# A dilated three-tap convolution with a gated activation: other operands for the warm-up products, and work pulled ahead of four places where TensorE waits

## The chip, the cores and the metric

The kernel runs on one core of a Trainium2 chip. The metric is the time of one execution on the device in microseconds (us), as the median of three runs. A core has TensorE (PE, the matrix products), VectorE (DVE), ScalarE (ACT), GpSimd (POOL), SyncE (SP, which issues most of the DMAs) and 16 DMA engines. Each engine works through its own list of instructions in order and waits on semaphores for the others.

## The reference

```python
def reference(x, w, w_o):          # x (2, 16000, 256), w (3, 256, 512), w_o (256, 256), all bf16
    dil = 2
    pad = (K - 1) * dil
    xp = jnp.pad(x, ((0, 0), (pad, 0), (0, 0)))
    h = jnp.einsum('btc,cd->btd', xp[:, pad:pad + T, :], w[0])
    for i in range(1, K):
        off = pad - i * dil
        h = h + jnp.einsum('btc,cd->btd', xp[:, off:off + T, :], w[i])
    f, g = h[..., :D], h[..., D:]
    z = jnp.tanh(f) * jax.nn.sigmoid(g)
    return z @ w_o
```

Every output row is made of three products of rows of `x` that lie two apart with a 256 x 512 weight, a tanh of one half times a sigmoid of the other, and one more product with a 256 x 256 weight.

## The kernel before

The time axis is cut into groups of rows. Most groups are wide: 256 columns of 8 rows each, read transposed by a DMA into a tile `xq`. A group is worked off in four blocks of 128 output channels, in the order 0, 2, 1, 3, so that a tanh block and its sigmoid block follow each other. The main loop goes over the blocks by number `k`; it starts at `k = ND = 4`, since blocks 0 to 3 belong to a first small group that is computed directly. There is also a small group `extra` (tiles `xte`, `e_ps`), whose four blocks are strewn into the loop at `k` = 4 to 7 by `extra_block`, and a small group `end` (`f_ps`).

The wide blocks save products. VectorE (and GpSimd for a part) first forms sums and differences of the input columns (`q`, `qp`, `qm`, `qd`), and each block then needs seven pairs of 512-column products. A block's PSUM tile `y` has two banks, and its steps follow each other across engines:

- `first` (weights `wmh`, two products, one for each half `ct` of the input channels) and ScalarE's copy `st` of the sum (`keep_first`),
- `second` (weights `wph`) and ScalarE's copy `sv` (`keep_second`), from which GpSimd makes `other`,
- `third` (weights `wm`), after which VectorE splits the bank into the second one (`split_bank`, L286),
- `late(B, 0)` in the next turn (weights `wt`, `wu`), which needs the split; then VectorE's `rest` (L290, `sv<-sv,y`), which needs these products,
- `late(B, 1)` (weights `wd2`, `wd0`, operand `qd`), which adds to the banks that `rest` has read and so needs `rest`,
- the activations on ScalarE, the gate (tanh times sigmoid, L339) on VectorE, and in a later turn the output products `out_mm` (L364), ScalarE's copy out of PSUM (L401) and the store.

`y` tiles come from a pool of three, the tiles `o_ps`, `e_ps` and `f_ps` from a pool of two. The order on each engine is the order of the calls in the loop; nothing is rescheduled. VectorE's steps other than `split_bank` and `rest` come from three tables by `k`: `small` and `big`, run early in a turn, and `mid`, which holds one step alone, `wide_m(G, 1)` of the second wide group at `k = 7`, which forms the second half of `qm` for the block that comes next.

At the start TensorE has no data yet. It runs products on a tile `warm` that VectorE sets to zero, L140, until the first 512 rows of `x` have come. These are transposed on TensorE (`turn`, L183) and copied to SBUF; from then on real products run (`direct`, L310), and VectorE forms the weight sums and the first `q`, `qp` and `qm`.

At the end of the list there are no blocks left to fill the waits: `late(V, 0)` of the last block, the projections that are left over (`project`, `left`), `late(V, 1)`, and the last group's projections, whose stores are issued one after the other by SP and ScalarE.

Of the kernel before, what the change touches and what calls it, by code (L numbers as in the profile page):

```python
# [13 lines left out]
def kernel(  # L14
# [23 lines left out]
    nc = tc.nc  # L38
    bf16 = mybir.dt.bfloat16
# [3 lines left out]
    P = 128  # L43
# [6 lines left out]
    BANK = 512  # L50
    O_ORDER = (0, 2, 1, 3)
    TAPS = (2, 0, 1)
# [4 lines left out]
    for b in range(B):  # L57
        t, stop = (4 * 2 * P if b == 0 else 0), (T - 4 * RE if b == B - 1 else T)
        while t < stop:
            n = min(need, (stop - t) // 8)  # L60
# [14 lines left out]
    consts = ctx.enter_context(tc.tile_pool(name="consts", bufs=1))  # L75
# [22 lines left out]

    def load_plain(G):
        b, r0, R = G["b"], G["r0"], G["R"]  # L100
# [22 lines left out]
            G["cols"].append((col + RH, slice(row, row + rows)))  # L123
            col, row = col + RH + rows, row + rows

    warm = consts.tile([P, BANK], bf16)
    nc.vector.memset(warm[:], 0.0)
    w_taps = [consts.tile([P, CT, D2], bf16, name=f"w{k}_sb") for k in range(K)]
    wo_sb = consts.tile([P, NT, D], bf16)
    xn = osb_pool.tile([P, 4, D], bf16, name="osb")  # L130
# [3 lines left out]
        nc.scalar.dma_start(out=w_taps[k][:], in_=w_in[k])  # L134
    nc.scalar.preload_act_table(ACT.Sigmoid)
    nc.sync.dma_start(out=w_taps[TAPS[1]][:], in_=w_in[TAPS[1]])
    for n in range(14):
        if n < 6 and n % 2 == 0:
            wps = new_y()
        nc.tensor.matmul(  # L140
            wps[:, 1, (n % 2) * 256:(n % 2 + 1) * 256], lhsT=warm[:, :P], rhs=warm[:, :256],
            start=n % 2 == 0 and n < 6, stop=True, skip_group_check=True,
        )
# [107 lines left out]
    def first(B, ct):  # L251
        if ct == 0:
            B.y = new_y()
        nc.tensor.matmul(  # L254
            B.y[:, 0, :], lhsT=W["wmh"][:, ct, B.osl], rhs=B.G["qp"][:, :, ct, :],
            start=ct == 0, stop=ct == CT - 1, skip_group_check=True,
        )
# [4 lines left out]
    def third(B):  # L262
        mm(B, W["wm"], B.G["qm"][:, 1], 0)

    def late(B, n):
        G = B.G
        if n == 0:
            mm(B, W["wt"], G["q"][:, 1, 0], 0)
            mm(B, W["wu"], G["q"][:, 1, 1], 1)
        else:  # L270
            mm(B, W["wd2"], G["qd"][:, 0], 0)
            mm(B, W["wd0"], G["qd"][:, 1], 1)
# [12 lines left out]
    def split_bank(B):  # L285
        nc.vector.scalar_tensor_tensor(  # L286
            out=B.y[:, 1, :], in0=B.st[:], scalar=-0.5, in1=B.y[:, 0, :], op0=ALU.mult, op1=ALU.add)
# [67 lines left out]
            return G["z"][:, dt, WIDE_PLACE[jp], lo:lo + P]  # L355
        return G["z"][:, dt, 2 * jp + q, rb0:rb0 + P]

    def out_mm(G, rb0, jp, o_ps=None):
        if o_ps is None:
            o_ps = ps_o.tile([P, 2, D], f32, name="o_ps", tag="o_ps")  # L360
        G["o", rb0, jp] = o_ps
        for q in range(2):
            for dt in range(NT):
                nc.tensor.matmul(  # L364
                    o_ps[q] if isinstance(o_ps, list) else o_ps[:, q, :], lhsT=z_columns(G, rb0, jp, q, dt), rhs=wo_sb[:, dt, :],
                    start=(dt == 0), stop=(dt == NT - 1),
                )

    def store(G, rb0, js, osb, queue=None):

        queue = queue or nc.sync
        if not G["wide"]:
            t0 = 4 * G["r0"] + 4 * rb0
            queue.dma_start(out=out[G["b"], t0:t0 + 4 * P, :].rearrange("(p j) d -> p j d", j=4)[:, js, :], in_=osb[:])
            return
        row = 0
        for b, t0, rows in G["parts"]:
            lo, hi = max(rb0, row), min(rb0 + P, row + rows)
            if lo < hi:
                t = t0 + 8 * (lo - row)  # L380
                queue.dma_start(
                    out=out[b, t:t + 8 * (hi - lo), :].rearrange("(p j) d -> p j d", j=8)[:, js, :],
                    in_=osb[lo - rb0:hi - rb0],
                )
            row += rows

    def out_evict(G, rb0, jp, on_dve):
        o_ps = G["o", rb0, jp]
        copy = nc.vector.tensor_copy if on_dve else nc.scalar.copy
        if jp is None:  # L390
            te = 4 * G["r0"]
            osb = consts.tile([P, 2, D], bf16, name="osb_end")
            copy(out=osb[:], in_=o_ps)
            rows = out[G["b"], te:te + 4 * RE, :].rearrange("(r q h) d -> h r q d", q=2, h=2)
            for h in range(2):
                nc.sync.dma_start(out=rows[h], in_=osb[h * RE:(h + 1) * RE])
            return
        h = jp % 2
        if h == 0:
            G["osb"] = osb_pool.tile([P, 4, D], bf16, name="osb")  # L400
        copy(out=G["osb"][:, 2 * h:2 * h + 2, :], in_=o_ps)  # L401
        if h == 1:
            store(G, rb0, slice(2 * jp - 2, 2 * jp + 2), G["osb"])


    blocks = [Block(G, oi) for G in groups for oi in range(4)]
    extras = [Block(extra, oi) for oi in range(4)]
    ends = [Block(end, oi) for oi in range(4)]
    ND = 4
# [47 lines left out]
    last = wide_m(G0, 1)  # L457

    def extra_block(i, taps):
        E = extras[i]  # L460
        if TAPS[0] in taps:
            E.y = ps_o.tile([P, BANK], f32, name="e_ps", tag="o_ps")
        direct(E, taps, E.y[:])
        if TAPS[-1] in taps:
            activate(E, E.y[:])
# [17 lines left out]
    ready, todo, made = [], [], []  # L483
    small, big, mid = {}, {}, {}

    def do(steps, k):
        ins = None
        for step in steps.pop(k, []):
            ins = step() or ins
        return ins  # L490
# [32 lines left out]
    def project(n):  # L523
        for piece in todo[:n]:
            out_mm(*piece)
            made.append(piece)
        del todo[:n]

    for k in range(ND, NB):
        B, V = blocks[k], (blocks[k - 1] if k > ND else None)  # L530

        E = {
            ND: [(0, TAPS[2:]), (1, TAPS[:1])], ND + 1: [(1, TAPS[2:])], ND + 2: [(2, TAPS)],
            ND + 3: [(3, TAPS)],
        }.get(k, [])
        early_second = k == ND + 1
        if early_second:
            second(B)
            keep_second(B)
            extra_block(1, TAPS[1:2])  # L540
        if V:
            late(V, 0)
        if k >= ND + 2:
            Y = blocks[k - 2]
            activate(Y, "y")
            note_gates(Y, k)
        last = do(small, k) or last

        if k == ND + 6:
            todo.append(ready.pop())  # L550
        big_late = k == ND + 1

        def big_and_quarter(last):
            last = do(big, k) or last
            if B.oi == 0 and k > ND:
                quarter(B.G, 3, last)
            elif B.oi and not big_late and B.G["n"] + 1 < len(wides):
                for i in range(0 if k == ND + 2 else B.oi - 1, B.oi):
                    quarter(wides[B.G["n"] + 1], i, last)
            return last  # L560

        if not big_late:
            last = big_and_quarter(last)
        if not early_second:
            second(B)
            keep_second(B)
        if k == ND:
            for i in range(2, ND):
                activate(blocks[i], bank(blocks[i], i))
        other(B, last)  # L570
        if V:
            rest(V)
        last = do(mid, k) or last
        for e in E:
            extra_block(*e)
        if k in (ND + 4, ND + 5):
            plain_ends(*((ACT.Sigmoid, 1) if k == ND + 5 else (ACT.Tanh, 0)))

        project(0 if k < ND + 3 else 1 if k < ND + 6 else 2)
        evict()  # L580
        N = blocks[k + 1] if ND < k < NB - 1 else None

        split_first = k >= ND + 2
        if N:
            first(N, 0)
            if not split_first:
                first(N, 1)
        third(B)
        split_bank(B)
        if k == ND + 3:  # L590
            last = gates_of(extra, slice(0, 2))
        if big_late:
            last = big_and_quarter(last)
        if V:
            activate(V, "sv")
        if N:
            if split_first:
                first(N, 1)
            keep_first(N)
        if V:  # L600
            late(V, 1)
        todo += ready
        ready.clear()
        if B.oi == 0:
            if loaded_wide < len(wides):
                load_wide(loaded_wide)
                loaded_wide += 1
            if k == ND:
                load_end()
# [2 lines left out]

    Y, V = blocks[NB - 2:]
    G = V.G
    late(V, 0)
    activate(Y, "y")
    big.pop(NB)
# [5 lines left out]
    gate_phases(0, slice(0, 2), nc.gpsimd)  # L623
    rest(V)
    gate_phases(0, slice(2, 4))
    project(2)
    evict()


# [5 lines left out]
    left = [todo[i:i + 2] for i in range(0, len(todo), 2)]  # L635
# [17 lines left out]

    activate(V, "sv")
    two_pieces(left[0], "y")
    out_evict(*left[0][0], True)
    late(V, 1)
    gate_phases(1, slice(2, 4))
    activate(V, "y")
    out_evict(*left[0][1], True)  # L660
    two_pieces(left[1], "o")
    last_mm(0, (1, 2), "y")
    gate_phases(1, slice(0, 2))
    out_evict(*left[1][0], False)
    out_evict(*left[1][1], False)
    last_mm(P, (1, 2), "y")
    last_evict(0, (1, 2), (nc.sync, nc.sync))
    last_mm(0, (0, 3), "o")
# [35 lines left out]
```

## Time and profile before

| | |
|---|---|
| median of three runs | 263.51 us (263.49 to 263.56) |
| the profiled execution | 263.43 us, of which the span from the first to the last instruction 261.6 us |
| PE busy | 256.0 us, 98% of the span |
| ACT busy | 245.9 us, 94% |
| DVE busy | 226.7 us, 87% |
| POOL busy | 112.8 us, 43% |
| chain of work that ended last | PE 93%, DVE 3% |

The median is 0.08 us above the profiled execution, and 1.8 us of that execution lie outside the span. A product's recorded time runs from its start to its end and overlaps that of the next one, so a busy share of 98% does not say how dense the products are. The gaps between the starts do.

### The profile page before, as it was taken

How to read it: one execution, taken by the hardware profiler on the slowest of the kernel's cores; microseconds unless marked ns; L12 is line 12 of the kernel's file. 1: busy time of each engine (PE TensorE's matmuls, PEld its weight loads, DVE VectorE, ACT ScalarE, POOL GpSimd, SP SyncE). 2: the span in 40 equal slices, each digit the busy share in tenths (PEclk: the TensorE clock that was granted, in tenths of full speed). 3: DMA queues.
4: the chain of work that ended last, by engine and by line, in shares of the span. 5: the costliest groups of instructions: out<-in, count | busy, mean ns of one | idle time of the engine just before them, and what ended most of it. 6: DMA issues, size and time to landing. Idle time of an engine off the chain costs nothing.

```text
span 261.6 us, 4231 instructions
## 1 busy us (share of the span) xinstructions
PE 256.0 (98%) x1464; PEld 144.2 (55%) x1464; DVE 226.7 (87%) x264; ACT 245.9 (94%) x378; POOL 112.8 (43%) x129
## 2 busy tenths in 40 slices
PE   8999999999999999999999999999999999999993
PEld 6644555555555555555555555555555555555562
DVE  2989969989889989999988988988988988986673
ACT  4668789999999999999999999999999999999993
POOL 1033434454453454355455355355345345444240
PEclk9999999999999999999999999999999999999998
DMA  7979073292834719256392934729274491221226
GB/s 209 201 177 192 0 180 94 83 209 83 175 119 123 209 52 212 111 117 174 96 175 105 199 120 103 203 79 215 81 169 124 101 231 43 80 83 40 82 80 241
DMA packets 79109, 35.10 MB, mean 134 GB/s; under 512 B 69232, under 2 KB 71536, under 8 KB 79088
## 3 DMA queue, kind: packets, MB, share of 16 engines
q1 hardware_dynamic: 77984, 33.92, 52.8%
q10 hardware_dynamic: 1104, 0.92, 1.1%
q8 instruction: 11, 0.18, 0.3%
q14 instruction: 10, 0.08, 0.1%
HBM read 1.18 MB, written 16.38 MB: 67 GB/s over the span
## 4 chain that ended last, share of the span: by engine, by line
PE 93%; DVE 3%; issue 1%; DMA 1%; ACT 0%; DVEq 0%; ACTq 0%
PE y L246 58%; PE o_ps L364 19%; PE y L254 9%; PE y L310 2%; PE y L140 1%; PE e_ps L310 1%; PE f_ps L310 1%; DVE sv L290 1%; DVE y L286 1%; DMA out_dram<-osb 1%; DVE qm L222 1%; PE wt_ps L171 0%; ACT osb L401 0%; PE y L364 0%; DVE osb L648 0%
## 5 line engine op out<-in xcount | busy, mean ns | idle before, releaser
L283 POOL TENSOR_TENSOR sv<-sv,st 128x512 f32<-128x512 f32 x60 | 76.4, 1274 | 23.9 <-ACT sv L280 22.2
L231 POOL TENSOR_TENSOR qd<-xq 128x256 bf16<-128x256 bf16 (+2 forms) x60 | 34.9, 585 | 114.2 <-DVE zw L339 55.4
L290 DVE TENSOR_TENSOR sv<-sv,y 128x1024 f32<-128x1024 f32 x60 | 72.7, 1212 | 3.8 <-PE y L246 3.7
L246 PE MATMUL y<-qd,wd_sb 128*128 128x512 bf16 x240 | 61.6, 379 | 0.1
L401 ACT CAST osb<-o_ps 128x512 bf16<-128x512 f32 x114 | 61.1, 591 | 0.2 <-PE o_ps L364 0.2
L286 DVE SCALAR_TENSOR_TENSOR y<-st,y 128x512 f32<-128x512 f32 x60 | 41.8, 696 | 21.9 <-PE y L246 19.6
L364 PE MATMUL o_ps<-wo_sb,zw 128*128 128x256 bf16 x450 | 58.4, 273 | 0.0
L364 PEld LDWEIGHTS <-zw 128*128 128x128 bf16 x480 | 47.0, 98 | 17.1
L254 PE MATMUL y<-qp,wmh_sb 128*128 128x512 bf16 x120 | 44.8, 379 | 0.0
L246 PEld LDWEIGHTS <-wd_sb 128*128 128x128 bf16 x240 | 23.5, 98 | 28.5 <-issue 0.6
L280 ACT ACTIVATE sv<-y 128x512 f32<-128x512 f32 x60 | 35.9, 598 | 1.4 <-PE y L246 1.1
L213 DVE TENSOR_TENSOR q<-xq 128x2048 bf16<-128x2048 bf16 (+2 forms) x32 | 36.8, 1155 | 0.0
L276 ACT ACTIVATE st<-y 128x512 f32<-128x512 f32 x60 | 36.3, 607 | 0.2 <-PE y L254 0.2
L246 PE MATMUL y<-q,wt_sb 128*128 128x512 bf16 x120 | 35.7, 379 | 0.2 <-DVE y L286 0.2
L246 PE MATMUL y<-qm,wph_sb 128*128 128x512 bf16 x120 | 35.7, 379 | 0.0
L246 PE MATMUL y<-qm,wm_sb 128*128 128x512 bf16 x120 | 35.7, 379 | 0.0
L246 PE MATMUL y<-q,wu_sb 128*128 128x512 bf16 x120 | 35.7, 379 | 0.0
L339 DVE TENSOR_TENSOR zw<-thw,sgw 128x2048 bf16<-128x2048 bf16 x28 | 34.1, 1217 | 0.0
L332 ACT ACTIVATE thw<-sv 128x1024 bf16<-128x1024 f32 x30 | 32.4, 1078 | 0.4 <-DVE sv L290 0.4
L332 ACT ACTIVATE sgw<-sv 128x1024 bf16<-128x1024 f32 x30 | 32.4, 1078 | 0.0
L334 ACT ACTIVATE sgw<-y 128x1024 bf16<-128x1024 f32 x30 | 31.3, 1043 | 0.1
L334 ACT ACTIVATE thw<-y 128x1024 bf16<-128x1024 f32 x30 | 31.3, 1044 | 0.0
(68 smaller groups left out, 178.8 us busy)
## 6 DMA issues: line engine op xcount, KB each, us to landing
out_dram<-osb SPq DMA_DIRECT2D x56, 256.0 KB, 2.1
out_dram<-osb SPq DMA_DIRECT2D x6, 128.0 KB, 2.2
w_sb<-in_w_dram ACTq DMA_DIRECT2D x2, 256.0 KB, 4.4
out_dram<-osb SPq DMA_DIRECT2D x2, 160.0 KB, 2.0
osb<-in_x_dram SPq DMA_DIRECT2D x1, 256.0 KB, 3.2
w_sb<-in_w_dram SPq DMA_DIRECT2D x1, 256.0 KB, 4.3
xq<-in_x_dram SPq DMA_TRANSPOSE x16, 7.2
out_dram<-osb ACTq DMA_DIRECT2D x2, 128.0 KB, 2.2
```

The source lines that it names most:

```text
L213: ins = nc.vector.tensor_tensor(out=sums(G, "q")[:, h, :, :, :, sl].rearrange("p h q ct r -> p h (q ct) r"), in0=s, in1=a, op=ALU.subtract ...
L246: nc.tensor.matmul(B.y[:, bank, :], lhsT=wmat[:, ct, B.osl], rhs=mv[:, :, ct, :], start=False, stop=ct == CT - 1, skip_group_check=True,)
L254: nc.tensor.matmul(B.y[:, 0, :], lhsT=W["wmh"][:, ct, B.osl], rhs=B.G["qp"][:, :, ct, :], start=ct == 0, stop=ct == CT - 1, skip_group_che ...
L276: nc.scalar.mul(B.st[:], B.y[:, 0, :], 4.0)
L280: nc.scalar.mul(B.sv[:, 0], B.y[:, 0, :], 2.0)
L283: after(nc.gpsimd.tensor_tensor(out=B.sv[:, 1], in0=B.sv[:, 0], in1=B.st[:], op=ALU.subtract), behind)
L286: nc.vector.scalar_tensor_tensor(out=B.y[:, 1, :], in0=B.st[:], scalar=-0.5, in1=B.y[:, 0, :], op0=ALU.mult, op1=ALU.add)
L290: nc.vector.tensor_tensor(out=B.sv[:], in0=B.sv[:], in1=B.y[:], op=ALU.subtract)
L332: nc.scalar.activation(out=dst[:, 2:4, :], in_=B.sv[:], func=func, scale=0.25)
L334: nc.scalar.activation(out=dst[:, 0:2, :], in_=B.y[:], func=func, scale=0.25)
L364: nc.tensor.matmul(o_ps[q] if isinstance(o_ps, list) else o_ps[:, q, :], lhsT=z_columns(G, rb0, jp, q, dt), rhs=wo_sb[:, dt, :], start=(dt ...
L401: copy(out=G["osb"][:, 2 * h:2 * h + 2, :], in_=o_ps)
```

## The change

The change has four parts.

1. The warm-up products read the program's constant one (`const-bfloat16-1.0`, one element per partition, which GpSimd sets before the engines are released, repeated along the row) instead of the tile `warm`; VectorE's memset goes, and with it TensorE's wait for it. There are 15 products instead of 14.
2. In turns `k` = 5 to 7 TensorE's work is in another order: in turn 5 `first(blocks[6], 0)` stands before `late(V, 0)`, and the first two products of the extra block 2 stand between `third` and `late(V, 1)`; the first two of the extra block 3 go from turn 7 to turn 6.
3. `do(mid, k)`, VectorE's `wide_m` of turn 7, stands behind `split_bank` instead of ahead of it.
4. At the end, half of the first left-over projection (two products) stands ahead of `late(V, 0)`. The four copies `left` are each stored when done (four stores of 128 KB) and no longer in pairs (two of 256 KB).

```diff
-    warm = consts.tile([P, BANK], bf16)
-    nc.vector.memset(warm[:], 0.0)
+    warm = nc.const_aps.tensor(1.0, [P, BANK], bf16)
...
-    for n in range(14):
+    for n in range(15):
...
-    def out_mm(G, rb0, jp, o_ps=None):
+    def out_mm(G, rb0, jp, o_ps=None, qs=(0, 1)):
...
-        for q in range(2):
+        for q in qs:
...
-    def out_evict(G, rb0, jp, on_dve):
+    def out_evict(G, rb0, jp, on_dve, single=False):
...
-        if h == 1:
+        if single:
+            store(G, rb0, slice(2 * jp, 2 * jp + 2), G["osb"][:, 2 * h:2 * h + 2])
+        elif h == 1:
             store(G, rb0, slice(2 * jp - 2, 2 * jp + 2), G["osb"])
...
-            ND: [(0, TAPS[2:]), (1, TAPS[:1])], ND + 1: [(1, TAPS[2:])], ND + 2: [(2, TAPS)],
-            ND + 3: [(3, TAPS)],
+            ND: [(0, TAPS[2:]), (1, TAPS[:1])], ND + 1: [(1, TAPS[2:])], ND + 2: [(2, TAPS[1:]), (3, TAPS[:1])],
+            ND + 3: [(3, TAPS[1:])],
...
             extra_block(1, TAPS[1:2])
+            first(blocks[k + 1], 0)
         if V:
             late(V, 0)
...
             rest(V)
-        last = do(mid, k) or last
         for e in E:
             extra_block(*e)
...
         if N:
-            first(N, 0)
+            if not early_second:
+                first(N, 0)
             if not split_first:
                 first(N, 1)
         third(B)
+        if early_second:
+            extra_block(2, TAPS[:1])
         split_bank(B)
+        last = do(mid, k) or last
...
     G = V.G
+    half = todo[0]
+    out_mm(*half, None, (0,))
     late(V, 0)
...
-    project(2)
+    out_mm(*half, half[0]["o", half[1], half[2]], (1,))
+    made.append(todo.pop(0))
+    project(1)
     evict()
...
-    out_evict(*left[0][0], True)
+    out_evict(*left[0][0], True, True)
```

The other three copies of `left` get the same last argument. The changed file is one line shorter ahead of the main body, so what is L246 before is L245 now.

In TensorE's list, turn 5, the wait for `rest` sits on the first product with `wd2`. Before:

```order
L246 MATMUL y_239<-qm_230,wm_sb_136 128x512
L246 LDWEIGHTS wd2_sb_133
L246 MATMUL y_234<-qd_249,wd2_sb_133 128x512 [waits DVE_49]
L246 LDWEIGHTS wd2_sb_133
L246 MATMUL y_234<-qd_249,wd2_sb_133 128x512
```

The same place now, with the first two products of the extra block 2 (`e_ps_299`):

```order
L245 MATMUL y_238<-qm_229,wm_sb_135 128x512
L309 LDWEIGHTS w2_sb_92
L309 MATMUL e_ps_299<-xte_127,w2_sb_92 128x512 [waits PE_49]
L309 LDWEIGHTS w2_sb_92
L309 MATMUL e_ps_299<-xte_127,w2_sb_92 128x512
L245 LDWEIGHTS wd2_sb_132
L245 MATMUL y_233<-qd_248,wd2_sb_132 128x512 [waits DVE_49]
```

Two products of 512 columns now stand between `third` and the product that waits for VectorE.

In VectorE's list, turns 7 and 8, before (`sv<-sv,y` is `rest`, `y<-st,y` is `split_bank`, `qm` is the step of the table `mid`, `z` and `zw` are gates):

```order
L290 TENSOR_TENSOR sv_326<-sv_326,y_295 128x1024 [waits PE_49,Pool_49]
L222 TENSOR_TENSOR qm_358<-q_301 128x1024 [waits DVE_49]
L286 SCALAR_TENSOR_TENSOR y_340<-st_347,y_340 128x512 [waits PE_49,Activation_49]
L339 TENSOR_TENSOR z_264<-th_262,sg_263 128x1024 [waits Activation_49]
L339 TENSOR_TENSOR zw_305<-thw_303,sgw_304 128x2048
L290 TENSOR_TENSOR sv_364<-sv_364,y_340 128x1024 [waits PE_49,Pool_49]
```

and now:

```order
L289 TENSOR_TENSOR sv_328<-sv_328,y_281 128x1024 [waits PE_49,Pool_49]
L285 SCALAR_TENSOR_TENSOR y_342<-st_349,y_342 128x512 [waits PE_49,Activation_49]
L221 TENSOR_TENSOR qm_360<-q_303 128x1024 [waits DVE_49]
L338 TENSOR_TENSOR z_263<-th_261,sg_262 128x1024 [waits Activation_49]
L338 TENSOR_TENSOR zw_307<-thw_305,sgw_306 128x2048
L289 TENSOR_TENSOR sv_366<-sv_366,y_342 128x1024 [waits PE_49,Pool_49]
```

The split and `qm` have changed places; the rest stands as it did.

In TensorE's list at the end, before, the last products of the last turn (`wd0`) are followed by `late(V, 0)`:

```order
L246 MATMUL y_2743<-qd_2552,wd0_sb_132 128x512
L246 LDWEIGHTS wt_sb_137
L246 MATMUL y_2785<-q_2554,wt_sb_137 128x512 [waits DVE_49]
L246 LDWEIGHTS wt_sb_137
L246 MATMUL y_2785<-q_2554,wt_sb_137 128x512
```

and now by two products of a projection:

```order
L245 MATMUL y_2742<-qd_2551,wd0_sb_131 128x512
L363 LDWEIGHTS zw_2583
L363 MATMUL o_ps_2830<-wo_sb_93,zw_2583 128x256 [waits Activation_49]
L363 LDWEIGHTS zw_2583
L363 MATMUL o_ps_2830<-wo_sb_93,zw_2583 128x256
L245 LDWEIGHTS wt_sb_136
L245 MATMUL y_2784<-q_2553,wt_sb_136 128x512 [waits DVE_49]
```

The product that waits for VectorE's split has two 256-column products ahead of it, which stood behind `late(V, 0)` before.

More of the change, by code (lines that the diff above doesn't have):

```diff
@@ L659 @@
     activate(V, "y")
-    out_evict(*left[0][1], True)
+    out_evict(*left[0][1], True, True)
     two_pieces(left[1], "o")
@@ L663 @@
     gate_phases(1, slice(0, 2))
-    out_evict(*left[1][0], False)
-    out_evict(*left[1][1], False)
+    out_evict(*left[1][0], False, True)
+    out_evict(*left[1][1], False, True)
     last_mm(P, (1, 2), "y")
```

## The prediction

> **What bounds the kernel.** I read the page first, the first line of its busy times and the engines' shares of the chain that ended last:
>
> ```profile
> PE 256.0 (98%) x1464; PEld 144.2 (55%) x1464; DVE 226.7 (87%) x264; ACT 245.9 (94%) x378; POOL 112.8 (43%) x129
> PE 93%; DVE 3%; issue 1%; DMA 1%; ACT 0%; DVEq 0%; ACTq 0%
> ```
>
> The chain is TensorE's own work. So an edit pays where TensorE stands still, and only there. Its records overlap, so the waits column shows little; I went through the timeline of PE alone and compared starts. First the spacing of 512-column products that wait for nothing: four of them last 1.03 us and one lasts 0.38 us, so starts lie (1.03 - 0.38) / 3 = 0.216 us apart. Timeline of PE around turns 5, 7 and 11 and the end (start, us, engine, line):
>
> ```profile
> 16.48 0.59 PE L310 MATMUL e_ps<-xte,w_sb 128*128 128x512 bf16 x2
> 17.06 0.59 PE L246 MATMUL y<-q,wt_sb 128*128 128x512 bf16 x2
> 18.79 0.59 PE L246 MATMUL y<-qm,wm_sb 128*128 128x512 bf16 x2
> 19.47 0.59 PE L246 MATMUL y<-qd,wd_sb 128*128 128x512 bf16 x2
> ...
> 27.91 0.59 PE L246 MATMUL y<-qm,wm_sb 128*128 128x512 bf16 x2
> 28.35 0.38 PE L254 MATMUL y<-qp,wmh_sb 128*128 128x512 bf16 x1
> 28.56 1.03 PE L246 MATMUL y<-qd,wd_sb 128*128 128x512 bf16 x4
> 29.76 0.59 PE L246 MATMUL y<-q,wt_sb 128*128 128x512 bf16 x2 [0.17 <-DVE y L286]
> ...
> 42.11 0.38 PE L254 MATMUL y<-qp,wmh_sb 128*128 128x512 bf16 x1
> 42.43 0.81 PE L246 MATMUL y<-qd,wd_sb 128*128 128x512 bf16 x3
> ...
> 248.46 1.02 PE L246 MATMUL y<-qd,wd_sb 128*128 128x512 bf16 x4
> 249.48 0.59 PE L246 MATMUL y<-q,wt_sb 128*128 128x512 bf16 x2
> ```
>
> Two products from 16.48 would hand over at 16.91; the next starts at 17.06: 0.15 us lost. In the same way 19.47 - (18.79 + 0.43) = 0.25, 29.76 - (28.56 + 0.86) = 0.34, 42.43 - (42.11 + 0.22) = 0.10 and 249.48 - (248.46 + 0.86) = 0.16 us. Who releases them stands in VectorE's rows:
>
> ```profile
> 16.31 0.69 DVE L286 SCALAR_TENSOR_TENSOR y<-st,y 128x512 f32<-128x512 f32 x1 [0.81 <-PE y L246]
> 18.19 1.22 DVE L290 TENSOR_TENSOR sv<-sv,y 128x1024 f32<-128x1024 f32 x1
> ...
> 26.56 1.20 DVE L290 TENSOR_TENSOR sv<-sv,y 128x1024 f32<-128x1024 f32 x1
> 27.69 1.42 DVE L222 TENSOR_TENSOR qm<-q 128x1024 bf16<-128x1024 bf16 x1
> 29.03 0.68 DVE L286 SCALAR_TENSOR_TENSOR y<-st,y 128x512 f32<-128x512 f32 x1
> 29.62 0.68 DVE L339 TENSOR_TENSOR z<-th,sg 128x1024 bf16<-128x1024 bf16 x1
> 30.23 1.21 DVE L339 TENSOR_TENSOR zw<-thw,sgw 128x2048 bf16<-128x2048 bf16 x1
> ```
>
> The split ends at 17.00, `rest` at 19.41, the next split at 29.71: each 0.05 to 0.06 us ahead of the product it releases. The third one was not late for TensorE's sake: `third` ended at 27.91 + 0.59 = 28.50, but VectorE was in `qm` until 29.11.
>
> **Turn 5.** The first stall gets one product (0.22), the second gets two (0.43), all taken from later places, so TensorE's total work is the same and what counts is whether the released work is still in time. By the spacing, with 0.11 for a 256-column product: `first` at 16.91, `late(4, 0)` 17.13, its last product ends at 17.13 + 0.65 + 0.38 = 18.16, before 18.19, when VectorE gets to `rest` anyway. So `rest` stays at about 18.2 and ends by 19.44. TensorE goes on with four products of extra 1 (0.44), the other half of `first` (0.22), `third` (0.43) and the two new ones (0.43), and arrives at `late(4, 1)` at 17.13 + 0.86 + 1.52 = 19.51, with `rest` done and 0.05 passed. Both stalls are covered, the second barely: 0.15 + 0.25 = 0.40.
>
> **Turns 6 and 7.** The extra blocks' four moved products even out: turn 6 gives two away and takes two in, so TensorE meets its VectorE steps there at nearly the old time, and the 0.40 shows in turn 7, which is two products shorter. `third` then ends near 28.50 - 0.40 = 28.10, `rest` ends at 27.8 as before, and the split, no longer behind `qm`, runs from 28.2 to 28.9. TensorE reaches `late(7, 0)` at 29.42 - 0.40 = 29.02: no wait, 0.34 gained, 0.74 in all. What is late next? Behind the split stand `qm`, `z`, `zw`, `rest`. `qm` alone is short, as at 12.35:
>
> ```profile
> 12.35 0.69 DVE L222 TENSOR_TENSOR qm<-q 128x1024 bf16<-128x1024 bf16 x1
> 27.29 1.27 POOL L283 TENSOR_TENSOR sv<-sv,st 128x512 f32<-128x512 f32 x1
> 33.66 1.03 PE L246 MATMUL y<-qd,wd_sb 128*128 128x512 bf16 x4
> ```
>
> From 28.8: `qm` to 29.5, `z` to 30.1, `zw` to 31.3, `rest` to 32.4. The product that waits for it comes at 33.66 - 0.74 = 32.92, half a us later. `qm` itself is first read by `third` of turn 8, past 32. From there on VectorE and ScalarE wait for TensorE and shift with it, so the 0.10 at 42.43 stays.
>
> `qm` took 1.42 where GpSimd's L283 ran from 27.29 to 28.56. The Trainium skill (SBUF — State Buffer, Who interferes with whom) says that a VectorE instruction with two SBUF inputs blocks against a GpSimd one that reads SBUF, for that one's whole length. By that rule `qm` would have ended near 28.56 + 0.69 = 29.25; the trace has 29.11, so it about agrees. In its new place `qm` starts some 0.2 us behind L283's end, and the rule costs nothing; it speaks for the first rival if that order turns.
>
> **The start.** Rows from the barrier to the first wide product, and the page's times to landing:
>
> ```profile
> 0.74 0.40 SPq L132 DMA_DIRECT2D osb<-in_x_dram  x1
> 0.86 0.27 DVE L127 MEMSET warm<- 128x256 uint32 x1 [0.86 <-PEq L688]
> 1.19 3.17 PE L140 MATMUL y<-warm 128*128 128x256 bf16 x14 [1.19 <-DVE warm L127]
> 1.20 0.42 SPq L136 DMA_DIRECT2D w_sb<-in_w_dram  x1
> 4.15 0.63 PE L183 MATMUL tp<-ident,osb 128*128 128x128 bf16 x4
> 5.66 1.22 DVE L428 TENSOR_TENSOR ws_sb<-w_sb 128x1024 f32<-128x1024 bf16 x1
> 11.74 0.69 DVE L219 TENSOR_TENSOR qp<-q 128x1024 bf16<-128x1024 bf16 x1
> 12.55 1.05 PE L254 MATMUL y<-qp,wmh_sb 128*128 128x512 bf16 x4
> ...
> osb<-in_x_dram SPq DMA_DIRECT2D x1, 256.0 KB, 3.2
> w_sb<-in_w_dram SPq DMA_DIRECT2D x1, 256.0 KB, 4.3
> ```
>
> Fourteen products spaced 0.211 (3.17 less one of 0.42, by 13) fill 1.19 to 4.15. Without the wait TensorE may begin at 0.74 to 0.86, as the other engines do; 15 products then end near 4.0. The rows of `x` land at 0.74 + 3.2 = 3.94. So the transposes come 0.1 to 0.2 earlier. Most of that is lost again: `ws_sb` needs the weight that lands at 1.20 + 4.3 = 5.5 and can move 0.1 at most, VectorE is busy from there to `qp`'s end at 12.43, and TensorE's wide product at 12.55 needs `qp`. I take 0.05, with bounds 0 and 0.17.
>
> **The end.** Two 256-column products (0.22) cover the 0.16. They need an `o_ps` tile that ScalarE has just emptied, in time. `late(V, 0)` starts 0.06 later, `rest` with it, and `late(V, 1)` 0.16 earlier. What then takes part of it back:
>
> ```profile
> 250.60 1.22 DVE L290 TENSOR_TENSOR sv<-sv,y 128x1024 f32<-128x1024 f32 x1 [1.17 <-PE y L246]
> 251.94 1.07 ACT L332 ACTIVATE sgw<-sv 128x1024 bf16<-128x1024 f32 x1
> 253.04 0.69 DVE L620 TENSOR_TENSOR zw<-thw,sgw 128x1024 bf16<-128x1024 bf16 x1
> 253.82 1.36 PE L364 MATMUL y<-wo_sb,zw 128*128 128x256 bf16 x11
> 255.66 3.02 SPq L649 DMA_DIRECT2D out_dram<-osb  x6
> ```
>
> The gate that ends at 253.73 depends on `rest` and ScalarE, which do not get earlier, so TensorE at 253.82 gains only about 0.06. The casts behind the second activation, which needs `late(V, 1)`, gain the whole 0.16, and SP's last six stores follow these. The two more stores cost SP about 0.5 each (3.02 / 6), but start from 253.0 instead of 254.4. I take 0.12 of the 0.16, with 0.06 below.
>
> **The sum.** 0.74 + 0.05 + 0.12 = 0.91 us off the profiled execution's 263.43 (span 261.6, the rest outside), so 262.52. The median of the runs is 0.08 higher: 262.60. With the bounds, 0.74 + 0.17 + 0.16 = 1.07 and, if turn 5 only half works, 0.54 + 0 + 0.06 = 0.60: 262.44 to 262.91. A measurement of this kernel can tell about 0.2%, 0.53 us, from no change.
>
> **Rivals.** *VectorE takes over* (0.12). From 16.9 to 23.6 it has no idle time, and turn 5's second cover has nothing to spare. If `qm` is blocked again (1.42 - 0.69 = 0.73), `rest` ends at 33.1 and TensorE stalls 0.25; if the second stall returns, it is 0.25 too. One of them gives 262.85, both 263.1.
>
> *The warm-up doesn't start earlier* (0.06), because TensorE isn't ready by 0.98 us, where 15 products end as 14 did. At worst the fifteenth pushes the transposes, VectorE's chain and the product at 12.55 by 0.21 less their 0.07 of slack: 0.14 lost for 0.05 gained, 262.8.
>
> *The clock rises later* (0.07): slower. The products' lengths tell it; `lines` of PE by form, before 6.5 us and from 7.2 on:
>
> ```profile
> L310 PE MATMUL y<-xt,w_sb 128*128 128x256 bf16 x7 | 1.7, 413 | 0.0
> ...
> L310 PE MATMUL y<-xt,w_sb 128*128 128x256 bf16 x7 | 0.9, 273 | 0.0
> ```
>
> TensorE runs at half pace until about 7, some 5.8 us behind the first warm-up product. If products on a repeated constant don't count as work, the 5.8 start with the transposes at 4.0: full pace at 9.8, 2.8 us at half pace, 1.4 us of products late, and all of it behind `qp`'s release. With 0.86 gained elsewhere that is 264.05. It decides once the rise is over 1.8 us late. Against it: the zeros counted. The Trainium skill (TensorE: Matmul & The Clock Gate, What's actually happening) speaks of free-running windows of about 3.4 us, one of them busy throughout, and of a warm-up budget in time, not in products. By that rule the earlier start moves the rise by a whole window or not at all; the trace's 5.8 us lies within one to two windows, and the sum stands either way, since `qp` holds TensorE.
>
> **Chances.** Forecast 0.70, the rivals 0.12, 0.06 and 0.07, and 0.05 for a loss I don't see. Faster: forecast, second rival and half of the first, 0.82; the same: the other half and most of the unseen, 0.10; slower: 0.08. The range 262.35 to 263.05 leaves out the slow clock, both stalls and the unseen.
>
> **What would show it.** PE starts 0.22 apart at the places of 17.06, 19.47 and 29.76, with the 0.10 kept near 41.6; the split of turn 7 ahead of a `qm` of 0.69; warm-up from about 0.8 and a full pace by 7; the last SP store about 0.1 nearer to the end of TensorE's work. A gap at the new `late(4, 1)` or a late `rest` in turn 8 would make the forecast wrong by 0.25 each, long warm-up products by more.

## The result, and the profile after

The changed kernel takes 262.87 us (median of 18 runs, 262.62 to 263.4), the kernel before on the same chip 263.51. The ratio is 0.9975, with a 95% interval of 0.9968 to 0.9981: 0.64 us faster, where 0.91 was forecast and 262.60 us. It lies within the range. The profiled execution took 263.09 us, span 261.3.

From the page after, the first line of the busy times and the engines' shares of the chain:

```profile
PE 254.6 (97%) x1465; PEld 143.4 (55%) x1465; DVE 225.5 (86%) x263; ACT 246.0 (94%) x378; POOL 112.9 (43%) x129
PE 92%; DMA 4%; DVE 1%; issue 0%; SPq 0%; ACT 0%; DVEq 0%; ACTq 0%
```

In the chain the DMA share has grown from 1% to 4%, and DVE's has shrunk from 3% to 1%. We come back to it.

**The middle.** Timeline of PE after, around turns 5 and 7 (start, us, engine, line):

```profile
16.80 0.59 PE L309 MATMUL e_ps<-xte,w_sb 128*128 128x512 bf16 x2
17.23 0.38 PE L253 MATMUL y<-qp,wmh_sb 128*128 128x512 bf16 x1
17.45 0.59 PE L245 MATMUL y<-q,wt_sb 128*128 128x512 bf16 x2
...
18.97 0.59 PE L245 MATMUL y<-qm,wm_sb 128*128 128x512 bf16 x2
19.40 0.60 PE L309 MATMUL e_ps<-xte,w_sb 128*128 128x512 bf16 x2
19.86 0.81 PE L245 MATMUL y<-qd,wd_sb 128*128 128x512 bf16 x3
...
28.51 1.03 PE L245 MATMUL y<-qd,wd_sb 128*128 128x512 bf16 x4
29.38 0.59 PE L245 MATMUL y<-q,wt_sb 128*128 128x512 bf16 x2
```

All starts are now 0.22 us times the number of products apart (16.80 + 0.43 = 17.23, + 0.22 = 17.45; 28.51 + 0.86 = 29.37). The one at 19.86 comes 0.03 late, where 0.25 were lost. And VectorE, in the same turn 7:

```profile
28.57 0.70 DVE L285 SCALAR_TENSOR_TENSOR y<-st,y 128x512 f32<-128x512 f32 x1 [0.51 <-ACT osb L400]
29.17 0.68 DVE L221 TENSOR_TENSOR qm<-q 128x1024 bf16<-128x1024 bf16 x1
```

The split stands ahead of a `qm` of 0.68 us. From the first wide product to `late(7, 0)` the kernel before took 29.76 - 12.55 = 17.21 us; this one takes 29.38 - 12.88 = 16.50. That is 0.71 saved, against 0.74 in the sum.

**The start.** Timelines of PE and of VectorE after:

```profile
0.78 3.19 PE L139 MATMUL y<-const-bfloat16-1.0 128*128 128x256 bf16 x15 [0.78 <-PEq L697]
3.81 0.38 PE L182 MATMUL tp<-ident,osb 128*128 128x128 bf16 x4
7.70 3.65 PE L309 MATMUL y<-xt,w_sb 128*128 128x512 bf16 x24
12.88 1.04 PE L253 MATMUL y<-qp,wmh_sb 128*128 128x512 bf16 x4 [1.54 <-DVE qp L218]
...
6.81 1.23 DVE L430 TENSOR_TENSOR wmh_sb<-ws_sb,w_sb 128x1024 bf16<-128x1024 f32 x1
10.87 1.23 DVE L212 TENSOR_TENSOR q<-xq 128x2048 bf16<-128x2048 bf16 x1 [0.51 <-DMA xq<-in_x_dram]
12.14 0.69 DVE L218 TENSOR_TENSOR qp<-q 128x1024 bf16<-128x1024 bf16 x1
```

The warm-up starts 0.4 earlier and the four transposes take 0.38 us together, where the kernel before took 0.63: full pace from 3.8 on. But the lead ends in a wait of 1.54 us for `qp`. VectorE in turn stood 0.51 us for the transposed load of `xq`, which is the DMA in the chain. The first wide product comes at 12.88, later than before's 12.55.

**The end.** PE's last rows and SP's last stores:

```profile
248.37 1.02 PE L245 MATMUL y<-qd,wd_sb 128*128 128x512 bf16 x4
249.24 0.38 PE L363 MATMUL o_ps<-wo_sb,zw 128*128 128x256 bf16 x2
249.45 0.59 PE L245 MATMUL y<-q,wt_sb 128*128 128x512 bf16 x2
...
253.58 1.91 PE L363 MATMUL y<-wo_sb,zw 128*128 128x256 bf16 x16
...
256.86 0.38 PE L363 MATMUL o_ps<-wo_sb,zw 128*128 128x256 bf16 x2
255.63 2.91 SPq L658 DMA_DIRECT2D out_dram<-osb  x6
```

The two products stand where the 0.16 was, and `wt` follows them by 0.21, without a wait. SP's last issue ends at 258.54, 1.30 behind PE's last product (257.24); in the kernel before these were 258.68 and 257.48, 1.20 apart. The prediction had this distance 0.1 shorter, and it is 0.1 longer.

**What nobody had named.** One long gap between starts is left that the kernel before doesn't have. After, near 210 us, VectorE and then PE:

```profile
208.04 1.21 DVE L289 TENSOR_TENSOR sv<-sv,y 128x1024 f32<-128x1024 f32 x1
209.94 0.70 DVE L285 SCALAR_TENSOR_TENSOR y<-st,y 128x512 f32<-128x512 f32 x1 [0.69 <-PE y L253]
...
209.53 1.03 PE L245 MATMUL y<-qd,wd_sb 128*128 128x512 bf16 x4
210.69 0.59 PE L245 MATMUL y<-q,wt_sb 128*128 128x512 bf16 x2
```

The same turn before:

```profile
208.42 1.21 DVE L290 TENSOR_TENSOR sv<-sv,y 128x1024 f32<-128x1024 f32 x1
209.97 0.70 DVE L286 SCALAR_TENSOR_TENSOR y<-st,y 128x512 f32<-128x512 f32 x1 [0.34 <-PE y L246]
...
209.91 1.03 PE L246 MATMUL y<-qd,wd_sb 128*128 128x512 bf16 x4
210.77 0.59 PE L246 MATMUL y<-q,wt_sb 128*128 128x512 bf16 x2
```

The split follows `rest` (208.04, 208.42) by 1.90 us instead of 1.55, an idle time of 0.69 instead of 0.34: 0.35 late. TensorE's `late(B, 0)` follows at 210.69, where 209.53 + 0.86 = 210.39 was due: 0.30 lost (0.29 with the trace's nanoseconds). The trace shows why this isn't a late product: the wait in front of the split is a record of its own and ends at 209.542, but the split starts 0.396 us behind it. At the 53 other splits between 35 and 245 us that have such a record, the median is 0.045 and none is over 0.06. Ahead of this place, the nearest step that the change moved is the `qm` at 29.17, 180 us earlier; behind it, the two products at 249.24.

### The profile page after: what moved, and what is told of

The parts are those of the page before. It is cut to its first block, busy times and chain, and to the rows that moved or that the text cites. A ratio compares the mean times of both kernels' runs of the same rounds, so it can differ in the third digit from the quotient of the medians.

```text
span 261.3 us, 4236 instructions
## 1 busy us (share of the span) xinstructions
PE 254.6 (97%) x1465; PEld 143.4 (55%) x1465; DVE 225.5 (86%) x263; ACT 246.0 (94%) x378; POOL 112.9 (43%) x129
## 4 chain that ended last, share of the span: by engine, by line
PE 92%; DMA 4%; DVE 1%; issue 0%; SPq 0%; ACT 0%; DVEq 0%; ACTq 0%
PE y L245 59%; PE o_ps L363 19%; PE y L253 10%; DMA xq<-in_x_dram 4%; PE e_ps L309 2%; PE y L363 1%; PE f_ps L309 1%; DVE q L212 0%; DVE osb L657 0%; DVE y L285 0%; DVE qp L218 0%; ACT osb L657 0%; SPq L135 0%; SPq L131 0%; DVEq L708 0%
## 5 line engine op out<-in xcount | busy, mean ns | idle before, releaser
L245 PE MATMUL y<-qd,wd_sb 128*128 128x512 bf16 x240 | 61.6, 379 | 0.0
L245 PEld LDWEIGHTS <-wd_sb 128*128 128x128 bf16 x240 | 23.5, 98 | 28.2 <-issue 0.2
L245 PE MATMUL y<-q,wt_sb 128*128 128x512 bf16 x120 | 35.7, 379 | 0.1
L245 PE MATMUL y<-qm,wph_sb 128*128 128x512 bf16 x120 | 35.7, 379 | 0.0
L245 PE MATMUL y<-qm,wm_sb 128*128 128x512 bf16 x120 | 35.7, 379 | 0.0
L245 PE MATMUL y<-q,wu_sb 128*128 128x512 bf16 x120 | 35.7, 379 | 0.0
```

The lines of the kernel that those rows point to most:

```text
L245: nc.tensor.matmul(B.y[:, bank, :], lhsT=wmat[:, ct, B.osl], rhs=mv[:, :, ct, :], start=False, stop=ct == CT - 1, skip_group_check=True,)
```

## The experiments

**Which part does it.** Each part alone, and all but the first. `e1_only_warm` is the kernel before with part 1, `e3_only_mid` with parts 2 and 3, `e4_only_end` with part 4; `e2_no_warm` is the changed kernel with the old warm-up:

```diff
-    warm = nc.const_aps.tensor(1.0, [P, BANK], bf16)
+    warm = consts.tile([P, BANK], bf16)
+    nc.vector.memset(warm[:], 0.0)
...
-    for n in range(15):
+    for n in range(14):
```

> The kernel before with the change of the warm-up alone (constant one, 15 products). In the changed kernel's trace TensorE reached full pace at 3.7 us, one window earlier, and then stood 1.7 us for qp, because q waited for xq, which landed at 10.85; the first wide product came at 12.88 (12.55 before). Theory: the first wide product is held by xq's landing and VectorE, whatever the warm-up does, and the 0.34 are the scatter of that landing: the time is within 0.15 us of before (263.4 to 263.65), and the first wide product starts between 12.4 and 12.9. Rival 1: the warm-up itself delays the start, through an earlier crowd on SBUF or the DMA engines: 0.25 to 0.4 us slower. Rival 2: the gain of the start does come through in most executions: 0.2 to 0.5 us faster.

> The changed kernel with the old warm-up (tile set by VectorE, 14 products). Theory: 0.72 (middle) + 0.12 (end) less than before, 262.65 to 262.8, and so about the same as the changed kernel. Rival 1 (the warm-up costs 0.3): 262.55, faster than the changed kernel by 0.3. Rival 2 (the warm-up gains): 262.9 to 263.1, slower than the changed kernel.

> The kernel before with the new order in turns 5 to 7 and the moved step of the table mid alone. Theory: the three waits of 0.15, 0.24 and 0.33 us are gone in the trace and the time falls by 0.65 to 0.75 us, 262.75 to 262.9. Rival: what TensorE gains in turns 5 to 7 is given back later, at a wait that comes up in the long middle (the changed kernel's trace has one of 0.29 us at 210.7): 0.3 to 0.5 us faster, and such a wait in this trace too.

> The kernel before with the change at the end alone (two products ahead of late(V, 0), four stores of 128 KB). Theory: the wait of 0.155 us goes; the end follows by 0.06 to 0.16 us: 263.35 to 263.45. Rival: the stores in halves hold SP and the last store, and nothing is gained, or up to 0.1 us lost: 263.5 to 263.6.

The kernel before ran at 263.49 us beside them. Measured:

| kernel | median, us | ratio, 95% interval | gap near 210 |
|---|---|---|---|
| e1_only_warm | 263.65 | 1.0014, 1.0005 to 1.0022 | 0.29 |
| e2_no_warm | 262.47 | 0.9968, 0.9956 to 0.9981 | none |
| e3_only_mid | 262.96 | 0.9978, 0.997 to 0.9987 | none |
| e4_only_end | 263.38 | 0.9998, 0.9989 to 1.0007 | none |

The warm-up part makes the kernel slower, and without it the change is 0.4 us better. The middle gives most of the gain. The end's 0.11 by medians can't be told from nothing, though the 0.16 gap is gone in `e4_only_end`'s trace as well. The gap near 210 goes with part 1. Timelines of VectorE and PE of `e1_only_warm`:

```profile
210.16 0.70 DVE L285 SCALAR_TENSOR_TENSOR y<-st,y 128x512 f32<-128x512 f32 x1 [0.69 <-PE y L253]
...
210.91 0.59 PE L245 MATMUL y<-q,wt_sb 128*128 128x512 bf16 x2
```

**What in part 1 does it.** Part 1 does four things: other operands, a fifteenth product, an earlier start, and one instruction less in VectorE's list. Theory 1 says it is the last: VectorE is held up at a fixed place of its list, in the kernel before that place fell on an instruction that was waiting anyway, and with the list one shorter it falls on the split. The rivals are the three changes to the warm-up itself. `e5_pad_front` adds a memset that nobody needs ahead of all else, `e6_pad_late` adds the same one ahead of the last block's products, and `e7_pool_memset` is the kernel before with the warm-up tile set by GpSimd:

```diff
+    pad = consts.tile([P, 16], bf16, name="pad")
+    nc.vector.memset(pad[:], 0.0)
...
-    nc.vector.memset(warm[:], 0.0)
+    nc.gpsimd.memset(warm[:], 0.0)
```

> The changed kernel with one more instruction ahead of everything else in VectorE's list: a memset of a 128x16 tile that nothing reads. The warm-up products still read the constant one and there are still fifteen. Theory 1 (place in the list): VectorE has one delay of about 0.35 us at a fixed place of its list; the removed memset let the split near 210 us slip onto that place. With the memset back in the count, the 0.29 us gap of TensorE near 210 goes, and the median is about 262.45 to 262.55. Theory 2 (the constant or the early start itself costs it): the gap near 210 stays, median about 262.85.

> The same extra memset, but at the end, ahead of the last block's products (near 249 us), so VectorE has as many instructions as in the kernel with the memset in front, only all up to 249 us stand one place earlier. Theory 1 (place in the list): the gap of 0.29 us near 210 stays, median about 262.85. Rival (the number of instructions in all, or how the program is laid out behind it): the gap goes or moves, about 262.5.

> The kernel before with one word changed: the warm-up tile is set by GpSimd and not by VectorE, so VectorE's list is one shorter and no constant is read; fourteen products. Theory 1 (place in the list): a gap of about 0.29 us appears near 210 us, and the median is about 263.8, 0.3 above the kernel before (a late or early start of the warm-up within 0.3 us does not count, since the first wide product waits for VectorE). Theory 2 (the constant or the early start): no gap near 210, about 263.5.

The kernel before ran at 263.46. `e5_pad_front`: 262.47 (ratio 0.9958, 0.9946 to 0.997). `e6_pad_late`: 262.81 (0.9972, 0.996 to 0.9984). `e7_pool_memset`: 263.84 (1.0013, 1.0005 to 1.0022). VectorE's split and the products of PE near 210, first `e5_pad_front`:

```profile
209.40 0.70 DVE L287 SCALAR_TENSOR_TENSOR y<-st,y 128x512 f32<-128x512 f32 x1 [0.34 <-PE y L247]
...
209.34 1.03 PE L247 MATMUL y<-qd,wd_sb 128*128 128x512 bf16 x4
210.21 0.59 PE L247 MATMUL y<-q,wt_sb 128*128 128x512 bf16 x2
```

then `e6_pad_late`:

```profile
209.67 0.70 DVE L285 SCALAR_TENSOR_TENSOR y<-st,y 128x512 f32<-128x512 f32 x1 [0.69 <-PE y L253]
...
209.27 1.03 PE L245 MATMUL y<-qd,wd_sb 128*128 128x512 bf16 x4
210.42 0.59 PE L245 MATMUL y<-q,wt_sb 128*128 128x512 bf16 x2
```

and `e7_pool_memset`:

```profile
210.28 0.70 DVE L286 SCALAR_TENSOR_TENSOR y<-st,y 128x512 f32<-128x512 f32 x1 [0.69 <-PE y L254]
...
209.88 1.02 PE L246 MATMUL y<-qd,wd_sb 128*128 128x512 bf16 x4
211.03 0.59 PE L246 MATMUL y<-q,wt_sb 128*128 128x512 bf16 x2
```

With the memset in front the products are 0.87 apart, no gap, although the constant, the fifteenth product and the early start are still there. With the same memset far behind they are 1.15 apart again. And the kernel before gets the gap when its list is one shorter, with no constant and no earlier warm-up. All three came as theory 1 had it, and the rivals fall.

**Two fewer.** If the place is fixed, one more instruction less should put it on `qp`, for which nobody waits. `e9_two_fewer` has ScalarE make one of two small tiles; `e10_after_again` is the changed kernel, unaltered, beside it:

```diff
-        nc.vector.tensor_scalar_mul(two[:], ident[:], -2.0 if i else 2.0)
+        (nc.scalar.mul if i else nc.vector.tensor_scalar_mul)(two[:], ident[:], -2.0 if i else 2.0)
```

> The changed kernel with one more instruction gone from VectorE's list ahead of 210 us: the second of the two small scaled identities (128x128) is made by ScalarE. VectorE's list is then two shorter than that of the kernel before. Theory 1 (one delay of some 0.35 us at a fixed place of the list): the place now falls on the instruction behind the split of the turn at 210 us, the step that forms qp, which starts while the split's 0.70 us still run and which nobody waits for; TensorE's gap of 0.29 goes, the median is about 262.5. Rival (a shorter list is hurt, wherever the place falls): the gap stays, about 262.85.

> The changed kernel as it is, for comparison on the same chip: the gap of 0.29 us near 210, median 262.8 to 262.9, and 0.3 to 0.4 above the kernel with two fewer if theory 1 holds.

Before: 263.53. `e9_two_fewer`: 262.90 (0.9977, 0.9968 to 0.9986); `e10_after_again`: 262.87 (0.9976, 0.9966 to 0.9985). The gap near 210 went, as expected, and the time stayed, which was not expected. The trace of `e9_two_fewer` has the answer, VectorE and PE near 46 and VectorE near 210:

```profile
46.16 0.70 DVE L285 SCALAR_TENSOR_TENSOR y<-st,y 128x512 f32<-128x512 f32 x1 [0.81 <-PE y L253]
...
45.69 1.03 PE L245 MATMUL y<-qd,wd_sb 128*128 128x512 bf16 x4
46.91 0.59 PE L245 MATMUL y<-q,wt_sb 128*128 128x512 bf16 x2 [0.20 <-DVE y L285]
...
209.69 0.70 DVE L285 SCALAR_TENSOR_TENSOR y<-st,y 128x512 f32<-128x512 f32 x1 [0.34 <-PE y L245]
```

There is a second such place. The split near 46 now starts 0.463 us behind its wait, and TensorE loses 46.91 - 45.69 - 0.86 = 0.36. In the order of VectorE's records in the trace, semaphore waits counted, this split is record 64, and the split near 210 is record 320 in all of `after`, `e1_only_warm`, `e6_pad_late`, `e7_pool_memset` and `e10_after_again`. In the other kernels no split is record 64 or 320, and none is late.

**Is it every 64th?** Two and three memsets in front of the changed kernel put a split on record 256, near 166.5, and on record 128, near 84.5:

```diff
+    for n in range(2):
+        nc.vector.memset(consts.tile([P, 16], bf16, name=f"pad{n}")[:], 0.0)
```

> The changed kernel with two more memsets of unread 128x16 tiles at the front of VectorE's list, one more than in e5. Counting VectorE's records in the trace, the delays seen so far struck a split at record 320 (four kernels) and at record 64 (e9). Theory 1a (a delay at every 64th record): the split of the turn near 166.5 us is now record 256, it starts some 0.35 us late, TensorE has a gap of about 0.29 there and none at 210; median about 262.8. Theory 1b (every 256th record, so 64 and 320 alone): no gap at 166 or 210, median about 262.45.

> The changed kernel with three more memsets of unread tiles at the front of VectorE's list. The split of the turn near 84.8 us is now record 128. Theory 1a (a delay at every 64th record): a gap of TensorE of about 0.3 us near 85, none elsewhere, median about 262.8. Theory 1b (records 64 and 320 alone): no such gap, median about 262.45.

Before: 263.42. `e11_two_more`: 262.48 (0.9961, 0.9949 to 0.9974). `e12_three_more`: 262.51 (0.9966, 0.9954 to 0.9979). The splits in question, from the timelines of VectorE of the one and of the other:

```profile
166.50 0.70 DVE L287 SCALAR_TENSOR_TENSOR y<-st,y 128x512 f32<-128x512 f32 x1 [0.34 <-PE y L247]
```

```profile
84.47 0.70 DVE L287 SCALAR_TENSOR_TENSOR y<-st,y 128x512 f32<-128x512 f32 x1 [0.34 <-PE y L247]
```

Both idle the usual 0.34. So not every 64th: 64 and 320 delay, 128 and 256 don't. Record 192 stays open, since in no kernel a split stands on it; what the trace shows of it stands in the last section.

**What holds the start.** `e8_pad_front_xq` is `e5_pad_front` with all tap weights loaded by ScalarE, so that SP gets to `xq` at once:

```diff
-    for k in (TAPS[0], TAPS[2]):
+    for k in TAPS:
         nc.scalar.dma_start(out=w_taps[k][:], in_=w_in[k])
...
-    nc.sync.dma_start(out=w_taps[TAPS[1]][:], in_=w_in[TAPS[1]])
```

> The changed kernel with the memset in front as in e5, and all three loads of the tap weights issued by ScalarE, so that SP issues the transposed load of the first wide group (xq) right behind that of the first rows, some 0.45 us earlier. Theory A (the landing of xq at 10.2 to 10.9 holds VectorE's q and so TensorE's first wide product at 12.4 to 12.9): xq lands 0.3 to 0.5 earlier, q starts when VectorE is ready near 10.38, TensorE's first wide product comes at 12.4 in every run, 0 to 0.3 below e5. Theory B (the weight sums are what is late: the weight then lands later on ScalarE's queue): VectorE's sums of the weights start later than 5.45 and the first wide product moves back by the same, 0.1 to 0.4 above e5.

Measured 266.37 us (1.0102, 1.0078 to 1.0125; single runs from 264.65 to 267.12), 3.9 above `e5_pad_front`. SP, VectorE and PE:

```profile
1.20 8.75 SPq L119 DMA_TRANSPOSE xq<-in_x_dram  x1
...
10.96 1.23 DVE L431 TENSOR_TENSOR wmh_sb<-ws_sb,w_sb 128x1024 bf16<-128x1024 f32 x1 [4.30 <-DMA w_sb<-in_w_dram]
14.44 1.22 DVE L213 TENSOR_TENSOR q<-xq 128x2048 bf16<-128x2048 bf16 x1
...
16.44 0.82 PE L254 MATMUL y<-qp,wmh_sb 128*128 128x512 bf16 x3 [1.02 <-DVE qp L219]
```

The load of `xq` does start 0.45 us earlier, but ScalarE's last weight, issued at 1.75 where it was 1.23, comes only at 10.9, VectorE waits 4.30 us for it, and the first wide product moves to 16.44. Theory B had the place right and the size wrong by a factor of ten, and theory A could not be read from this run. That `xq` holds the start rests on the rows where VectorE is idle for it, not on this experiment.

**The best version** is the changed kernel with the memset in VectorE's list again, or with the old warm-up: 262.47 in `e5_pad_front` and in `e2_no_warm`, 0.4 below the changed kernel and 1.0 below the kernel before.

## Why the prediction was right, and where it wasn't

**The middle, 0.74: right, step by step.** 0.71 in the traces. The second cover in turn 5 has nothing to spare, as said, and 0.03 shows there. `qm` takes 0.68 in its new place at 29.17, behind the GpSimd step (27.59 to 28.86), where it took 1.42 beside it: the rule of the Trainium skill (SBUF — State Buffer, Who interferes with whom) and the row agree. The first rival's stalls don't appear: `rest` of turn 8 ends at 32.73, and the product that needs it starts at 33.28, without a gap. The gap of 0.10 near 42 stayed, also as said.

**The start, 0.05: the term that was mis-sized, and of the wrong sign.** Two things lie in it. The earlier warm-up gave nothing that can be told: with the list's length restored, `e5_pad_front` (early start, constant) and `e2_no_warm` (old warm-up) have the same 262.47, each with an interval of about 0.3 us to either side. The traces say more: leaving out `e8_pad_front_xq`, whose start is another, the first wide product starts between 12.39 and 12.88 in the eight profiles with the new warm-up and between 12.42 and 12.59 in the five with a tile. So the bound of 0 was the right end. In the first profile the step waited not for VectorE's work alone but for `xq`. The same changed kernel, in another execution (`e10_after_again`, VectorE and PE):

```profile
10.56 1.23 DVE L212 TENSOR_TENSOR q<-xq 128x2048 bf16<-128x2048 bf16 x1
...
12.57 1.04 PE L253 MATMUL y<-qp,wmh_sb 128*128 128x512 bf16 x4 [0.80 <-DVE qp L218]
```

There `q` starts 0.31 earlier than in the first profile and the first wide product 0.31 earlier with it. The 12.88 was this execution's and not the change's. What the prediction didn't have is the price of taking an instruction out of VectorE's list. It counted the memset only as the wait at the start, and no step asked what stands some 320 records further on.

**How the sum comes out.** Gains over the kernel before by medians, in the four versions of the whole middle and end whose split isn't struck (`e2_no_warm`, `e5_pad_front`, `e11_two_more`, `e12_three_more`): 1.02, 0.99, 0.94 and 0.91, mean 0.97. In the four that have a struck split (`after`, `e6_pad_late`, `e9_two_fewer`, `e10_after_again`): 0.64, 0.65, 0.63 and 0.66, mean 0.65. The difference, 0.32, is the 0.29 to 0.36 that PE stands there. So the forecast of 0.91 was about right for what it counted, and the missing 0.27 has this one cause.

The traces give the same sum by stretches, again without `e8_pad_front_xq`. From the first wide product to `late(7, 0)` it is 17.21 us with the old order and 16.50 with the new one. From there to the last turn's `wd2` products it is 218.70 to 218.71 without a struck split, 218.99 to 219.00 with one at record 320 and 219.06 with one at record 64. From there to the end of the span it is 13.16 to 13.20 with the old end and 12.93 to 12.95 with the new one. So the middle brought 0.71, the end about 0.24 and the start nothing, 0.95 together. That 0.91 comes so near is in part luck: the end's term was 0.12 too small, and the other two together 0.08 too large.

The prediction kept 0.05 of its chances for a loss it didn't see, and its range was not to hold one. Such a loss is what came; that the time still lies in the range, because 0.27 is less than the 0.45 left above the forecast, is luck.

**The end, 0.12 with 0.06 below.** The gap closed. The step that let TensorE at 253.82 gain only 0.06 was too careful: from the last turn's `wd2` to these products it was 253.82 - 248.46 = 5.36 and is 253.58 - 248.37 = 5.21, so the whole 0.15 came through. From the end of PE's last product to the end of the span it is 4.07 us now and was 4.16, another 0.09, although SP's last issue comes later behind that product than before; what is shorter behind it stays open. By medians the part alone is too small to be told from none (0.9989 to 1.0007). That the parts measured alone add up to less than the whole (0.53 + 0.11 by medians against 1.02 for `e2_no_warm`) lies within their intervals, 0.2 to 0.35 us to either side.

**The rivals.** The warm-up did start earlier (0.78). The clock didn't rise later: products on a constant count, since the transposes at 3.81 run at full pace. In `e5_pad_front` the same fifteen products on the same constant did not bring full pace that early; its transposes (PE):

```profile
3.93 0.63 PE L184 MATMUL tp<-ident,osb 128*128 128x128 bf16 x4
```

Four of them took 0.63, the half pace of the kernel before. The unaltered changed kernel did the same in `e10_after_again`, where the four started at 3.93 and took 0.63, against 0.38 in the first profile. The Trainium skill's free-running windows (TensorE: Matmul & The Clock Gate, What's actually happening) would make one kernel differ so between executions, and the rows agree. As the prediction said, it decides nothing, since `qp` holds TensorE afterwards.

## What to carry to other kernels

An instruction has a place as well as a price: adding or removing one far off the critical path shifts all that follow on that engine against whatever holds the engine up at fixed places, and this can cost as much as the edit was to bring. When a part of a change loses and its own region of the trace looks better, compare the spacing of starts over the whole span for a new gap; then pad the list by one in front of the gap and by one behind it, which tells a place from a cause. And before speeding up a start, look for which arrival the first real work waits: the 0.4 us gained here, ahead of a load and of VectorE's chain, did not move the first wide product.

## What the runs showed of the hardware

VectorE is held up for 0.35 to 0.42 us at record 64 and at record 320 of its list, and not at 128 and 256: this shows in the six profiles in which a split stands at 64 or 320 and in the two with a split at 128 or 256. Where `rest` stands at record 64 (`before`, `e2_no_warm`, `e3_only_mid`, `e4_only_end`, `e5_pad_front`, `e8_pad_front_xq`), it starts 0.01 to 0.03 us before its predecessor's record ends, where 0.08 is usual: the same hold-up, as it seems, nearly hidden behind an instruction that still runs. What it is, the trace doesn't say. It lists transfers of instructions; queue 14 over the whole span of `after`, from the page's list of DMA queues:

```profile
q14 instruction: 11, 0.08, 0.1%
```

Ten of these are of 8 KB. In every profile one of them starts while VectorE is between records 62 and 66, one at record 191 or 192, and one between records 319 and 325. Where the list is longer or shorter they come earlier or later with it (the second at 124.48 in `e12_three_more`, at 127.26 in `e9_two_fewer`). None goes with records 128 and 256 in this way. That speaks for a refill of VectorE's list at places 128 apart, and record 192 would then be such a place too.

The Trainium skill (Runtime: NRT & Kernel Launch, Instruction fetch mechanics) says that an engine's instructions are refilled in blocks of 256 (16 KiB) while the program runs and that crossing a block costs "one DMA tail-bump, mostly hidden". The spacing of 256 doesn't agree with these transfers, which are half as large and 128 records apart. "Mostly" agrees: where the hold-up wasn't hidden, it was 0.3 us of 263. That the refill is the cause was not tested, and neither was an effect of the profiler, which writes these records.

A plain load of 256 KB that ScalarE issued at 1.75, 0.55 us behind the start of SP's transposed load (1.20), took 9.1 us to land (`e8_pad_front_xq`). In `e5_pad_front`, where all three weights are issued ahead of the transposed load (1.65), the slowest took 5.3. The step of VectorE that needs it began at 10.96 and at 7.22. The order of issue across the two queues decided 3.9 us; whether the transposed load did it or the place behind two other weights on ScalarE's queue was not tested.
